# Attention and expert routing in one kernel: expert embedding prepared at the start, idle matmuls redistributed, the last expert's w2 in column halves, the last router on VectorE

## The chip, the cores and the metric

The kernel runs on one core of a Trainium2 chip. A core has a matrix engine (TensorE, "PE" in the profile, with its weight loads as "PEld"), VectorE ("DVE"), ScalarE ("ACT"), GpSimd ("POOL") and SyncE ("SP", which here only issues transfers), and 16 DMA engines that serve all of them. Each engine runs its own list of instructions in order and waits on semaphores for the others. The metric is the device time of one execution in microseconds; the number for a kernel is the median of its runs.

## What is computed

The reference is an attention with an extra 1 in the softmax sum, followed by a layer of eight experts of which every token uses one:

```python
batch, n_heads, seq, head_dim = 8, 12, 448, 64          # attention
N, D, E, F = 3584, 768, 8, 1024                          # tokens, width, experts, hidden

scores = scale * np.matmul(q, k.transpose(0, 1, 3, 2))
m = np.max(scores, axis=-1, keepdims=True)
e = np.exp(scores - m)
attn = e / (np.sum(e, axis=-1, keepdims=True) + np.exp(-m) + 1e-09)
x = np.matmul(attn, v)                                   # then (B, S, H*D), flattened to (N, D)

xn = x / (np.linalg.norm(x, axis=-1, keepdims=True) + 1e-06)
en = expert_emb / (np.linalg.norm(expert_emb, axis=-1, keepdims=True) + 1e-06)
logits = xn @ en.T / tau
expert_idx = np.argmax(logits, axis=1)                   # one expert for each token
# gate_w = softmax(logits) at expert_idx
out[mask] = gate_w[mask, None] * (np.maximum(x[mask] @ w1[e], 0.0) @ w2[e])   # for each e
```

All inputs are float32. For each batch of 448 tokens the kernel finds the expert that most of its tokens chose, fetches only that expert's w1 and w2 (GpSimd's DMA casts them to bf16) and computes the whole batch with it. Tokens that chose another expert are handled afterwards by a loop that is entered only if there are any; with these inputs nothing of it shows in the profile.

## The kernel before

Heads are handled in pairs, 6 pairs for a batch, 48 in all. The program is written as a list of pieces of work, each put at a position; a pair has a slot of 8 positions (`NSLOT = 8`). The pieces are sorted by position, and so the order of the instructions on each engine follows. Attention runs alone for the first eleven slots; from then on the experts of a finished batch are computed between the matmuls of the later pairs. Nothing is left to overlap with the last batch's expert.

The constants and the expert embedding. `prep_expert_emb` is called at position 4 and `prep_expert_emb_t` in slot 5; the scaled embedding is needed when the first batch is routed, in slot 7:

```python
    emb = k.wp.tile([E, DM], F32, name="emb_raw", tag="w1")
    nc.sync.dma_start(emb[:], k.emb[:, :])
    ss = k.csp.tile([E, 1], F32, name="emb_ss", tag="cs")
    nrm = k.csp.tile([E, 1], F32, name="emb_nrm", tag="cs")

    def sq():
        sq = k.wp.tile([E, DM], F32, name="emb_sq", tag="w1")
        nc.scalar.activation(sq[:], emb[:], ACT.Square, accum_out=ss[:])

    def root():
        nc.gpsimd.tensor_tensor(out=nrm[:], in0=ss[:], in1=k.half[0:E, 0:1], op=ALU.pow)

    def ens():
        nc.vector.tensor_scalar_add(nrm[:], nrm[:], 1e-6)
        rs = k.csp.tile([E, 1], F32, name="emb_rs", tag="cs")
        nc.vector.reciprocal(out=rs[:], in_=nrm[:])
        nc.vector.tensor_scalar_mul(rs[:], rs[:], 1.0 / float(tau))
        k.ens = k.wp.tile([E, DM], F32, name="emb_scaled", tag="w1")
        nc.vector.tensor_scalar_mul(k.ens[:], emb[:], rs[:])

    k.en = k.const.tile([128, NP, 32], F32, name="en")
    k.put(s + 19.9, lambda: nc.vector.memset(k.en[:], 0.0))
    k.put(s + 20.8, sq)
    k.put(s + 24.5, root)
    k.put(s + 34.9, ens)


def prep_expert_emb_t(k, s):
    nc = k.nc
    tp = k.work.tile([128, 512], F32, name="work", tag="work")
    for c in range(NP):
        nc.tensor.transpose(tp[:, c * E : c * E + E], k.ens[:, 128 * c : 128 * c + 128], k.ident[:E, :E])

    def out():
        nc.vector.tensor_copy(
            out=k.en[:, :, 0:E], in_=tp[:, 0 : NP * E].rearrange("p (c e) -> p c e", e=E)
        )

    k.put(s + 1, out)

```

The first load. `nc.sync` and `nc.scalar` are the two queues that issue it:

```python
    else:   # in load_qk, for the first two pairs
        for h in range(0, 2 * GP, 2):
            for eng, dst, src in ((nc.sync, t.qm, k.q), (nc.scalar, t.km, k.k)):
                for j in range(2):
                    eng.dma_start(dst[:, :, h + j, :], src[0, h + j, 0:SM, :].rearrange("(p t) d -> p t d", t=3))
            for j, src in ((0, k.q), (1, k.k)):
                nc.sync.dma_start(t.r[64 * j : 64 * j + 64, h : h + 2, :], src[0, h : h + 2, SM:S, :].rearrange("h p d -> p h d"))
    k.ld[n] = t
```

The pieces for a pair, with their positions (`scores` makes four blocks of scores, their exp on ScalarE and the subtraction of 1 on VectorE; `attend` is the product with v; `recip` takes 1/(sum + 1) as exp(-ln)), and the idle matmuls, which compute nothing that is used (`warm(k, n)` issues n matmuls of 128x128 by 512 columns):

```python
    for g in range(G):
        s = g * NSLOT
        put(s - NSLOT + 4.2, lambda g=g, s=s - NSLOT + 4.2: front_qk(k, g, s))
        put(s + (0.8 if g else 4.85), lambda g=g: front_v(k, g))
        for j, o, pa, pv in ((0, 0, 0.3, 1.5), (1, 0.05, 0.4, 2.6), (2, 5.2, 6, 7.7), (3, 0.12, 2.3, 2.7 if g else 4.9)):
            put(s + o, lambda g=g, j=j, pa=s + pa, pv=s + pv: scores(k, g, j, pa, pv))

        s += NSLOT
        put(s + 0.1, lambda g=g, s=s: attend(k, g, s + 0.1))
        put(s + 4.75, lambda g=g, s=s: normalise(k, g, s + 4.75))
        put(s + (4.9 if g == G - 1 else NSLOT + 4.26 if on_pool(g) else NSLOT + 2.35), lambda g=g: square(k, g))
        if 0 < g % NP < NP - 1:
            p = not on_pool(g) and g < G - 2
            put(s + NSLOT + (2.6 if g == G - 2 else 4.28 if p else NSLOT + 0.6), lambda g=g, p=p: square_add(k, g, p))
    put(-NSLOT, lambda: warm(k, 15))
    for g in range(LAG):
        for o in (2.8, 5.4):
            put(g * NSLOT + o, lambda: warm(k, 3))
    for b in range(B):
        s = ((b + 1) * NP + 1) * NSLOT
        if b == B - 1:
            last_batch(k, G * NSLOT)
            break
        put(s + 2.85, lambda b=b, s=s: router_mm(k, b, s + 4.65))
        put(s + 5.35, lambda b=b, s=s: router_tok(k, b, s + 6.9))
```

```python
    def recip():   # in attend
        nc.scalar.activation(rd[:], ps[:, :, 0:S], ACT.Ln, bias=1.0, scale=1.0 / (S + 1.0))
        nc.scalar.activation(rd[:], rd[:], ACT.Exp, scale=-1.0)
```

The router of a batch: `router_mm` multiplies x with the embedding and sums the squares, `router_tok` turns the result so that tokens lie on partitions, and then:

```python
    m = p.tile([128, 4], F32, name="m", tag="m")
    nc.vector.reduce_max(out=m[:], in_=l[:], axis=AX.X)

    nc.gpsimd.tensor_tensor(out=l[:], in0=l[:], in1=m[:].unsqueeze(2).broadcast_to([128, 4, E]), op=ALU.subtract)
    oh = p.tile([128, 4, E], F32, name="oh", tag="oh")
    nc.gpsimd.tensor_scalar(out=oh[:], in0=l[:], scalar1=0.0, scalar2=None, op0=ALU.is_equal)
    ohb = p.tile([128, 4, E], BF16, name="ohb", tag="ohb")
    nc.gpsimd.tensor_tensor(out=ohb[:], in0=oh[:], in1=k.mask[:], op=ALU.mult)
    k.ohb[b], k.lg[b] = ohb, (l, nrm)
```

`router_pick` counts the tokens of each expert with a matmul of ones by `ohb`, `router_count` finds the most frequent expert, `router_index` loads its number into a register of GpSimd, and `fetch` loads a piece of the weights:

```python
def w_piece(k, e0, i):
    if i < 3:
        ...   # a piece of w1
    else:
        w = k.wp.tile([128, 2, DM], BF16, name="w2", tag="w2", bufs=8)
        src = k.w2[bass.ds(e0, 1), :, :].rearrange("o (f p) m -> p (o f) m", p=128)[:, 2 * i - 6 : 2 * i - 4, :]
    k.nc.gpsimd.dma_start(w[:], src)
    return w
```

The last batch fetches w1 in four column blocks (`fetch_columns`) and w2 by `fetch`, in four row blocks of 256 rows each. A hidden block is `moe_h` (6 matmuls for one of 8 blocks of 128 hidden units), an output tile is `moe_y` (128 tokens by 384 columns, 8 matmuls, one for each hidden block) or `moe_yr` (the last 64 tokens, both column halves, 16 matmuls):

```python
        nc.tensor.matmul(   # in moe_y
            ps[:, 0:SM], lhsT=hs[f][:, 128 * t : 128 * t + 128], rhs=w2[f // 2][:, f % 2, SM * n : SM * n + SM],
            start=(f == 0), stop=(f == NF - 1),
        )
    # ... the order of a batch's pieces, in moe_chunks:
    return [h(f) for f in range(NF)] + [y(0, 0), y(0, 1), yr, y(1, 0), y(1, 1), y(2, 0), y(2, 1)]
```

```python
def last_batch(k, s):
    # cut: b, put
    at = [s + o for o in (-5.2, -2.7, -2.6, 0.5, 1.0, 1.5, 5.5, 6.5)] + [s + 7.5 + 0.5 * i for i in range(22)]
    out = {0: (s - 3.4, True), 1: (s - 1.0, False), 2: (s + 0.5, True), 3: (s + 0.95, True), 4: (s + 2.5, False),
           5: (s + 4.8, True), 6: (s + 5.9, True), 7: (s + 6.6, False)}
    for i, fn in enumerate(moe_chunks(k, b - 1, s + 13.5) + moe_chunks(k, b)):
        put(at[i], lambda fn=fn, l=out.get(i, (at[i] + 0.45, i % 2 == 1)): fn(*l))
    # ... router_mm at s + 5.0 to router_index at s + 7.2
    for i in range(4):
        put(s + 7.3, lambda i=i: fetch_columns(k, b, i))
        put(s + 7.9, lambda i=i: fetch(k, b, 3 + i))
    # ... the rest of the gate
```

## Time and profile before

| | |
|---|---|
| time, median of 3 runs | 401.76 us (400.56 to 402.38) |
| span of the profiled execution | 400.7 us |
| TensorE, VectorE, ScalarE, GpSimd busy | 96%, 76%, 75%, 53% |
| data moved by DMA | 69.74 MB, mean 174 GB/s |
| chain that ended last, by engine | PE 75%, DVE 12%, POOL 4%, DMA 3%, issue 3%, ACT 2% |

How to read it. "L287" is line 287 of the kernel. A line of the timeline gives the start, the duration (of all instructions merged into the line), engine, source line, operation, output and inputs by name, and in brackets how long the engine had been idle before it and what released it. In the slices each digit is a fortieth of the span (10 us) in tenths; PEclk is the granted clock of TensorE. The costliest groups of the page are the exp of the scores (ScalarE, 144 instructions of 917 ns), the subtraction of 1 (VectorE, 144 of 631 ns) and the matmuls of the experts (384 of 326 ns and 336 of 356 ns; consecutive matmuls overlap).

### The profile page before, as it was taken

Reading aid. Unit: us, or ns where it says so; the run is one execution under the profiler, and the core shown is the slowest. Engines: PE = TensorE matmul, PEld = TensorE weight load, DVE = VectorE, ACT = ScalarE, POOL = GpSimd, SP = SyncE. Lnnn points to the kernel's source line nnn. Section 1 sums busy time; section 2 is a strip of 40 time slices with the busy share of each in tenths; the row PEclk is TensorE's granted clock in tenths of the full one; section 3 lists DMA queues with packets and bytes.
Section 4 is the critical chain, followed back from the end, with each engine's and each line's share of the span. In section 5 each row is a group of like instructions: output and inputs, shape, how many; then the busy total and the mean of one; then the engine's idle time right before and its main releaser. Section 6 shows DMA issues by size and latency. Waiting matters only on the chain.

```text
span 400.7 us, 7192 instructions
## 1 busy us (share of the span) xinstructions
PE 383.0 (96%) x2303; PEld 238.9 (60%) x2303; DVE 305.2 (76%) x678; ACT 299.2 (75%) x438; POOL 210.6 (53%) x302
## 2 busy tenths in 40 slices
PE   7999999899999999999999999999999999999975
PEld 3565565565666656665666656765666656655533
DVE  2789979967978878887978878887888888762311
ACT  1898889677888788787887887887887887852211
POOL 1423339943677248752776258651876349624800
PEclk9999999789999999999999999999999999999999
DMA  5878648998399959999499949999599808952993
GB/s 129 198 180 203 153 108 164 203 186 173 61 232 241 214 126 175 244 213 216 97 217 245 234 100 187 262 197 224 91 235 217 188 2 152 215 89 37 189 247 122
DMA packets 135688, 69.74 MB, mean 174 GB/s; under 512 B 99544, under 2 KB 130264, under 8 KB 135648
## 3 DMA queue, kind: packets, MB, share of 16 engines
q1 hardware_dynamic: 115344, 43.69, 43.1%
q0 software_dynamic: 18704, 25.17, 38.7%
q10 hardware_dynamic: 1600, 0.39, 0.4%
q8 instruction: 19, 0.31, 0.3%
q14 instruction: 21, 0.17, 0.2%
HBM read 83.39 MB, written 16.52 MB: 249 GB/s over the span
## 4 chain that ended last, share of the span: by engine, by line
PE 75%; DVE 12%; POOL 4%; DMA 3%; issue 3%; ACT 2%; POOLq 0%; DVEq 0%
PE work L528 16%; PE work L558 14%; PE av L287 12%; PE big L243 9%; DVE x L309 4%; PE tq L202 4%; PE work L249 4%; PE rmm L353 3%; PE tk L202 3%; DMA w<-in_moe_w_dram 3%; PE work L684 3%; PE work L577 2%; PE av L278 2%; DVE qt L213 2%; ACT e L254 1%
## 5 line engine op out<-in xcount | busy, mean ns | idle before, releaser
L254 ACT ACTIVATE e<-big 128x896 f32<-128x896 f32 x144 | 126.4, 917 | 30.3 <-PE big L243 29.9
L262 DVE TENSOR_SCALAR em<-e 128x896 fp32r<-128x896 f32 x144 | 89.5, 631 | 9.9 <-ACT e L254 6.9
L558 PE MATMUL work<-w,h 128*128 128x384 bf16 x384 | 68.6, 326 | 3.6 <-DMA w<-in_moe_w_dram 2.7
L528 PE MATMUL work<-xb,w 128*128 128x448 bf16 x336 | 71.4, 356 | 0.3 <-DVE h L537 0.3
L309 DVE SCALAR_TENSOR_TENSOR x<-av,rd 64x448 f32<-64x448 f32 x96 | 66.3, 691 | 2.9 <-ACT rd L296 0.7
L287 PE MATMUL av<-em,vab 128*128 128x448 f32 x288 | 67.6, 370 | 0.0
L243 PE MATMUL big<-qt,kt 64*128 64x448 f32 x288 | 58.3, 441 | 3.7 <-DVE kt L217 2.1
L287 PEld LDWEIGHTS av<-em,vab 128*128 128x128 f32 x288 | 54.8, 191 | 4.5 <-DVE em L262 0.4
L191 POOL TENSOR_TENSOR vs<-vs,vld 128x256 f32<-128x256 f32 x48 | 35.6, 742 | 37.3 <-ACT xs L334 19.1
L558 PEld LDWEIGHTS <-h 128*128 128x128 bf16 x384 | 36.0, 100 | 30.3 <-issue 9.8
L295 ACT ACTIVATE rd<-av 128x896 f32<-128x896 f32 x48 | 44.4, 925 | 6.9 <-PE av L292 6.4
L528 PEld LDWEIGHTS <-w 128*128 128x128 bf16 x336 | 31.7, 103 | 29.7 <-issue 6.7
L296 ACT ACTIVATE rd<-rd 128x896 f32<-128x896 f32 x48 | 45.7, 952 | 1.5
L537 DVE TENSOR_SCALAR h<-work 128x448 bf16<-128x448 f32 x45 | 28.1, 625 | 24.1 <-PE work L528 22.7
L213 DVE CAST qt<-tq 128x448 fp32r<-128x448 f32 x48 | 29.7, 618 | 20.2 <-PE tq L204 20.0
L191 POOL TENSOR_TENSOR vs<-vld 128x256 f32<-128x256 f32 x24 | 18.4, 768 | 49.8 <-PE av L292 33.0
L481 POOL DMA_DIRECT2D w<-in_moe_w_dram x53 | 41.3, 779 | 6.1 <-DVE h L537 2.7
L243 PEld LDWEIGHTS big<-qt,kt 64*128 64x128 f32 x288 | 24.2, 184 | 31.8 <-ACT e L254 10.1
L548 DVE TENSOR_SCALAR y<-work,g 128x384 f32<-128x384 f32 x31 | 19.2, 618 | 26.3 <-PE work L558 20.2
L550 ACT ACTIVATE y<-work,g 128x384 f32<-128x384 f32 x25 | 14.5, 581 | 25.1 <-PE work L558 20.6
L209 ACT CAST kt<-tk 128x384 fp32r<-128x384 f32 x48 | 22.4, 468 | 12.8 <-PE tk L202 12.8
L341 POOL TENSOR_TENSOR acc<-acc,xs 128x448 f32<-128x448 f32 x24 | 27.2, 1135 | 0.9 <-DVE emx L265 0.9
(108 smaller groups left out, 565.0 us busy)
## 6 DMA issues: line engine op xcount, KB each, us to landing
w<-in_moe_w_dram POOLq DMA_DIRECT2D x32, 384.0 KB, 6.5
w<-in_moe_w_dram POOLq DMA_DIRECT2D x21, 512.0 KB, 7.3
vld<-in_v_dram SPq DMA_DIRECT2D x24, 384.0 KB, 5.7
out_dram<-y SPq DMA_DIRECT2D x48, 192.0 KB, 6.1
qm<-in_q_dram SPq DMA_DIRECT2D x69, 128.0 KB, 3.8
km<-in_k_dram SPq DMA_DIRECT2D x69, 128.0 KB, 5.4
vld<-in_v_dram SPq DMA_DIRECT2D x48, 32.0 KB, 4.7
out_dram<-y SPq DMA_DIRECT2D x16, 96.0 KB, 6.5
```

What stands on the lines that cost most here:

```text
L191: k.behind(nc.gpsimd.tensor_tensor(out=vs[:], in0=(vs[:] if j > 1 else t.v[:, :, 0, :]), in1=t.v[:, :, j, :], op=ALU.add))
L213: nc.vector.tensor_copy(out=qt[:], in_=pq[:, 0:S])
L243: nc.tensor.matmul(ps[:, h, 0:S], lhsT=kt[64 * h : 64 * h + 64, 128 * j : 128 * j + 128], rhs=qt[64 * h : 64 * h + 64, :], start=True, sto ...
L254: nc.scalar.activation(e[:], ps[:, :, 0:S], ACT.Exp, scale=scale)
L262: k.last = nc.vector.tensor_scalar_sub(em[:], e[:], 1.0)
L287: nc.tensor.matmul(ps[:, h, 0:S], lhsT=va[:, j, h : h + 2, :], rhs=k.ems[g, j][:, h, :], start=False, stop=(j == 2),)
L295: nc.scalar.activation(rd[:], ps[:, :, 0:S], ACT.Ln, bias=1.0, scale=1.0 / (S + 1.0))
L296: nc.scalar.activation(rd[:], rd[:], ACT.Exp, scale=-1.0)
L309: nc.vector.scalar_tensor_tensor(out=x[r, :], in0=ps[r, h, 0:S], scalar=ps[r, 0, S : S + 1], in1=rd[o, h, :], op0=ALU.add, op1=ALU.mult,)
L481: k.nc.gpsimd.dma_start(w[:], src)
L528: nc.tensor.matmul(ps[:, 0:S], lhsT=(w1[c // 2][:, c % 2, 128 * f : 128 * f + 128] if len(w1) == 3 else w1[f // 2][:, c, 128 * (f % 2) : 1 ...
L558: nc.tensor.matmul(ps[:, 0:SM], lhsT=hs[f][:, 128 * t : 128 * t + 128], rhs=w2[f // 2][:, f % 2, SM * n : SM * n + SM], start=(f == 0), st ...
```

## The change

It touches the irregular places of the schedule and leaves the rest alone.

- The expert embedding is loaded at the very start by GpSimd's queue, and its norm, scaling and transposition are done in slots -1 and 0, while the first loads land, instead of in slots 3 to 5. Its constants are set earlier.
- One of the first loads (the remainder of k, rows 384 to 447) moves from SyncE's to ScalarE's queue.
- Idle matmuls: 10 in place of 15 at the start; none in slot 0 at the place where the embedding is now transposed; none in slot 7, where the first router runs; 8 in place of 3 in the second place of slot 10, just before the first expert starts.
- In slot 0 the second subtraction of 1 goes behind the next pair's copies.
- For the last pair `recip` works on each head by itself; the squares of the last two pairs are put earlier.
- For the last batch the router's three operations for the one-hot of the best expert run on VectorE in place of GpSimd.
- For the last batch w2 is fetched as (column half, row half) in place of four row blocks, and the output tiles of the first column half come first.

The diff, with cuts marked:

```diff
--- before.py
+++ after.py
@@ -41,6 +41,10 @@
     make_identity(nc, k.ident[:])
     k.ones_f = pool.tile([128, 1], F32, name="ones_f")
     nc.vector.memset(k.ones_f[:], 1.0)
+    k.half = pool.tile([128, 4], F32, name="half")
+    nc.vector.memset(k.half[:], 0.5)
+    k.en = pool.tile([128, NP, 32], F32, name="en")
+    nc.vector.memset(k.en[:], 0.0)
     iota_i = pool.tile([128, E], I32, name="iota_i")
     nc.gpsimd.iota(iota_i[:], pattern=[[1, E]], base=0, channel_multiplier=0)
     row_i = pool.tile([128, 1], I32, name="row_i")
# cut: two hunks that only take k.half out of its old place; further down, the one that uses w2_part in moe_yr
@@ -100,7 +102,7 @@
 def prep_expert_emb(k, s):
     nc, tau = k.nc, k.tau
     emb = k.wp.tile([E, DM], F32, name="emb_raw", tag="w1")
-    nc.sync.dma_start(emb[:], k.emb[:, :])
+    nc.gpsimd.dma_start(emb[:], k.emb[:, :])
     ss = k.csp.tile([E, 1], F32, name="emb_ss", tag="cs")
     nrm = k.csp.tile([E, 1], F32, name="emb_nrm", tag="cs")
 
@@ -119,11 +121,9 @@
         k.ens = k.wp.tile([E, DM], F32, name="emb_scaled", tag="w1")
         nc.vector.tensor_scalar_mul(k.ens[:], emb[:], rs[:])
 
-    k.en = k.const.tile([128, NP, 32], F32, name="en")
-    k.put(s + 19.9, lambda: nc.vector.memset(k.en[:], 0.0))
-    k.put(s + 20.8, sq)
-    k.put(s + 24.5, root)
-    k.put(s + 34.9, ens)
+    k.put(s + 0.5, sq)
+    k.put(s + 0.6, root)
+    k.put(s + 4.8, ens)
 
 
 def prep_expert_emb_t(k, s):
@@ -137,7 +137,7 @@
             out=k.en[:, :, 0:E], in_=tp[:, 0 : NP * E].rearrange("p (c e) -> p c e", e=E)
         )
 
-    k.put(s + 1, out)
+    k.put(s + 2.15, out)
 
 
 def load_qk(k, n):
@@ -163,8 +163,8 @@
             for eng, dst, src in ((nc.sync, t.qm, k.q), (nc.scalar, t.km, k.k)):
                 for j in range(2):
                     eng.dma_start(dst[:, :, h + j, :], src[0, h + j, 0:SM, :].rearrange("(p t) d -> p t d", t=3))
-            for j, src in ((0, k.q), (1, k.k)):
-                nc.sync.dma_start(t.r[64 * j : 64 * j + 64, h : h + 2, :], src[0, h : h + 2, SM:S, :].rearrange("h p d -> p h d"))
+            for j, eng, src in ((0, nc.sync, k.q), (1, nc.sync if h else nc.scalar, k.k)):
+                eng.dma_start(t.r[64 * j : 64 * j + 64, h : h + 2, :], src[0, h : h + 2, SM:S, :].rearrange("h p d -> p h d"))
     k.ld[n] = t
 
 
@@ -292,8 +292,11 @@
         nc.tensor.matmul(ps[:, 0, S : S + 1], lhsT=k.va[g // GP][:, 2 * i : 2 * i + 2, :], rhs=k.ones_f[:], start=True, stop=True)
 
     def recip():
-        nc.scalar.activation(rd[:], ps[:, :, 0:S], ACT.Ln, bias=1.0, scale=1.0 / (S + 1.0))
-        nc.scalar.activation(rd[:], rd[:], ACT.Exp, scale=-1.0)
+        parts = (slice(0, 1), slice(1, 2)) if g == B * NP - 1 else (slice(0, 2),)
+        for h in parts:
+            nc.scalar.activation(rd[:, h, :], ps[:, h, 0:S], ACT.Ln, bias=1.0, scale=1.0 / (S + 1.0))
+        for h in parts:
+            nc.scalar.activation(rd[:, h, :], rd[:, h, :], ACT.Exp, scale=-1.0)
 
     k.put(s + 0.04, rest)
     k.put(s + 2.3, recip)
@@ -380,11 +383,12 @@
     m = p.tile([128, 4], F32, name="m", tag="m")
     nc.vector.reduce_max(out=m[:], in_=l[:], axis=AX.X)
 
-    nc.gpsimd.tensor_tensor(out=l[:], in0=l[:], in1=m[:].unsqueeze(2).broadcast_to([128, 4, E]), op=ALU.subtract)
+    eng = nc.vector if b == B - 1 else nc.gpsimd
+    eng.tensor_tensor(out=l[:], in0=l[:], in1=m[:].unsqueeze(2).broadcast_to([128, 4, E]), op=ALU.subtract)
     oh = p.tile([128, 4, E], F32, name="oh", tag="oh")
-    nc.gpsimd.tensor_scalar(out=oh[:], in0=l[:], scalar1=0.0, scalar2=None, op0=ALU.is_equal)
+    eng.tensor_scalar(out=oh[:], in0=l[:], scalar1=0.0, scalar2=None, op0=ALU.is_equal)
     ohb = p.tile([128, 4, E], BF16, name="ohb", tag="ohb")
-    nc.gpsimd.tensor_tensor(out=ohb[:], in0=oh[:], in1=k.mask[:], op=ALU.mult)
+    eng.tensor_tensor(out=ohb[:], in0=oh[:], in1=k.mask[:], op=ALU.mult)
     k.ohb[b], k.lg[b] = ohb, (l, nrm)
 
 
@@ -494,6 +498,20 @@
     k.wts[b][0].append(w)
 
 
+def fetch_halves(k, b, i):
+    w = k.wp.tile([128, NF // 2, SM], BF16, name="w2c", tag="w2", bufs=8)
+    src = k.w2[bass.ds(k.e0[b], 1), :, :].rearrange("o (f p) m -> p (o f) m", p=128)
+    n, j = i // 2, i % 2
+    k.nc.gpsimd.dma_start(w[:], src[:, NF // 2 * j : NF // 2 * (j + 1), SM * n : SM * n + SM])
+    k.wts[b][1].append(w)
+
+
+def w2_part(w2, f, n):
+    if w2[0].shape[2] == SM:
+        return w2[2 * n + f // (NF // 2)][:, f % (NF // 2), :]
+    return w2[f // 2][:, f % 2, SM * n : SM * n + SM]
+
+
 def keep_rows(k, b):
 
     nc = k.nc
@@ -556,7 +574,7 @@
     ps = k.work.tile([128, 512], F32, name="work", tag="work")
     for f in range(NF):
         nc.tensor.matmul(
-            ps[:, 0:SM], lhsT=hs[f][:, 128 * t : 128 * t + 128], rhs=w2[f // 2][:, f % 2, SM * n : SM * n + SM],
+            ps[:, 0:SM], lhsT=hs[f][:, 128 * t : 128 * t + 128], rhs=w2_part(w2, f, n),
             start=(f == 0), stop=(f == NF - 1),
         )
 
@@ -626,6 +644,8 @@
                lambda n, y: send(s + 1, k.out[b * S + SM : b * S + S, SM * n : SM * n + SM], y),
                lambda fn: k.put(s, fn), vec)
 
+    if b == B - 1:
+        return [h(f) for f in range(NF)] + [y(0, 0), y(1, 0), y(2, 0), yr, y(0, 1), y(1, 1), y(2, 1)]
     return [h(f) for f in range(NF)] + [y(0, 0), y(0, 1), yr, y(1, 0), y(1, 1), y(2, 0), y(2, 1)]
 
 
@@ -700,7 +720,7 @@
     put(s + 7.2, lambda: router_index(k, b))
     for i in range(4):
         put(s + 7.3, lambda i=i: fetch_columns(k, b, i))
-        put(s + 7.9, lambda i=i: fetch(k, b, 3 + i))
+        put(s + 7.9, lambda i=i: fetch_halves(k, b, i))
     put(s + 7.4, lambda: router_first(k, b))
     put(s + 7.5, lambda: router_pow(k, b))
     put(s + 7.6, lambda: router_exp(k, b))
@@ -732,8 +752,8 @@
     k.hev = {}
     k.behind = behind
     put(4.6, lambda: build_late_consts(k))
-    put(4, lambda: prep_expert_emb(k, 4))
-    put(5 * NSLOT + 2.7, lambda: prep_expert_emb_t(k, 5 * NSLOT + 2.7))
+    put(-NSLOT, lambda: prep_expert_emb(k, -NSLOT))
+    put(2.8, lambda: prep_expert_emb_t(k, 2.8))
     for n in range(NG * B):
         s = n * GP * NSLOT
         put(max(-NSLOT, s - 6 * NSLOT + 5.2), lambda n=n: load_qk(k, n))
@@ -747,20 +767,21 @@
         s = g * NSLOT
         put(s - NSLOT + 4.2, lambda g=g, s=s - NSLOT + 4.2: front_qk(k, g, s))
         put(s + (0.8 if g else 4.85), lambda g=g: front_v(k, g))
-        for j, o, pa, pv in ((0, 0, 0.3, 1.5), (1, 0.05, 0.4, 2.6), (2, 5.2, 6, 7.7), (3, 0.12, 2.3, 2.7 if g else 4.9)):
+        for j, o, pa, pv in ((0, 0, 0.3, 1.5), (1, 0.05, 0.4, 2.6 if g else 4.86), (2, 5.2, 6, 7.7), (3, 0.12, 2.3, 2.7 if g else 4.9)):
             put(s + o, lambda g=g, j=j, pa=s + pa, pv=s + pv: scores(k, g, j, pa, pv))
 
         s += NSLOT
         put(s + 0.1, lambda g=g, s=s: attend(k, g, s + 0.1))
         put(s + 4.75, lambda g=g, s=s: normalise(k, g, s + 4.75))
-        put(s + (4.9 if g == G - 1 else NSLOT + 4.26 if on_pool(g) else NSLOT + 2.35), lambda g=g: square(k, g))
+        put(s + (4.9 if g == G - 1 else NSLOT + (4.26 if on_pool(g) else 0.3 if g == G - 2 else 2.35)), lambda g=g: square(k, g))
         if 0 < g % NP < NP - 1:
             p = not on_pool(g) and g < G - 2
-            put(s + NSLOT + (2.6 if g == G - 2 else 4.28 if p else NSLOT + 0.6), lambda g=g, p=p: square_add(k, g, p))
-    put(-NSLOT, lambda: warm(k, 15))
+            put(s + NSLOT + (0.9 if g == G - 2 else 4.28 if p else NSLOT + 0.6), lambda g=g, p=p: square_add(k, g, p))
+    put(-NSLOT, lambda: warm(k, 10))
     for g in range(LAG):
         for o in (2.8, 5.4):
-            put(g * NSLOT + o, lambda: warm(k, 3))
+            if g != NP + 1 and (g, o) != (0, 2.8):
+                put(g * NSLOT + o, lambda n=(8 if (g, o) == (LAG - 1, 5.4) else 3): warm(k, n))
     for b in range(B):
         s = ((b + 1) * NP + 1) * NSLOT
         if b == B - 1:
```

## The prediction, made before the changed kernel ran

> **What bounds the kernel now.** I read the page first (busy shares and the 40 slices), then the chain of waits in order of time, then the timeline of five stretches that the change touches. TensorE is busy 96% of the span and carries 75% of the chain, but a share says nothing of a stage, so I split the span by the `Ln` instruction (line 295), which runs once per head pair. Its starts in the timeline of ScalarE give the pace: 16.73, 22.39, 28.24, 33.84, 40.10, 46.47, 52.12, 59.56, 65.63, 71.30, 80.22, 89.15, then a steady cycle of six pairs in 44.65 us (89.15 to 133.80, 133.80 to 178.43). So there are three regimes: attention alone up to about 72 us at 5.66 us a pair, a disturbed handover, and from 89 us the mixed steady state. The change leaves the steady state alone; it touches irregular places only.
>
> The slices show the handover as the only place where the clock drops:
>
> ```profile
> PE   7999999899999999999999999999999999999975
> PEclk9999999789999999999999999999999999999999
> ```
>
> The windows put it at 0.66 of full clock from 74 to 80 us:
>
> ```profile
> 68.00:74.00 6.00, 5.66 (x31) 3.54 (x30) 5.89 (x12) 5.68 (x9) 5.59 (x6) 1.00 1.10 227
> 74.00:80.00 6.00, 4.36 (x15) 3.34 (x16) 5.63 (x13) 2.65 (x4) 5.76 (x9) 0.66 1.09 200
> ```
>
> (columns: length, then PE, PEld, DVE, ACT, POOL busy, clock, DMA share, GB/s: DVE and POOL are full before the clock falls.) The timeline, start and duration first, bracket = idle before and releaser, carries the rest:
>
> ```profile
> 1.67 6.36 PE L684 MATMUL work<-ident 128*128 128x512 bf16 x15 [1.67 <-POOL ident masks.py:199]
> 5.95 0.62 SPq L167 DMA_DIRECT2D qkrest<-in_q_dram  x1
> 7.87 0.49 PE L202 MATMUL tq<-ident,qm 128*128 128x128 f32 x3
> ...
> 38.08 0.61 DVE L120 TENSOR_SCALAR emb_scaled<-emb_raw,emb_rs 8x768 f32<-8x768 f32 x1
> 39.32 0.55 ACT L256 ACTIVATE e<-work 128x448 f32<-128x448 f32 x1 [0.75 <-DVE em L262]
> ...
> 51.94 0.81 PE L684 MATMUL work<-ident 128*128 128x512 bf16 x3
> 55.01 0.62 DVE L213 CAST qt<-tq 128x448 fp32r<-128x448 f32 x1 [1.98 <-PE tq L204]
> ...
> 74.97 0.67 PE L243 MATMUL big<-qt,kt 64*128 64x448 f32 x4 [1.12 <-DVE kt L217]
> 76.31 0.74 PE L278 MATMUL av<-emx,vab 64*128 64x448 f32 x2 [0.67 <-DVE x L309]
> 77.52 2.44 PE L287 MATMUL av<-em,vab 128*128 128x448 f32 x6
> 80.04 2.40 PE L528 MATMUL work<-xb,w 128*128 128x448 bf16 x6
> ...
> 364.29 0.18 PE L444 MATMUL pick<-ohb,ones_b 128*128 128x32 bf16 x1 [0.22 <-POOL ohb L387]
> 372.19 2.76 PE L558 MATMUL work<-w,h 128*128 128x384 bf16 x16 [0.56 <-DVE y L548]
> 385.03 0.48 PE L558 MATMUL work<-w,h 128*128 128x384 bf16 x2 [0.34 <-DMA w<-in_moe_w_dram]
> 387.88 1.79 PE L558 MATMUL work<-w,h 128*128 128x384 bf16 x10 [2.37 <-DMA w<-in_moe_w_dram]
> ```
>
> The reader is to see: the 15 idle matmuls end just when the first transpose starts; the embedding work makes ScalarE wait; in the router's slot VectorE waits for a TensorE that runs idle matmuls; six L287 matmuls take 2.44 us where they otherwise take 1.39; and the last expert waits 2.7 us for w2.
>
> [...] an idle matmul takes 0.43 us in the first 6 us and 0.22 us later, and the half-clock stretch runs from 76.3 to about 82.8 us. [...] The trace has 0.62 us per issue on SyncE, so that is what moving one load can save directly. [...] The trace: 0.23, 0.31, 0.25 us on GpSimd against 0.15 to 0.2 for the small VectorE operations beside them.
>
> **The change part by part.**
>
> Start. Five idle matmuls at 0.427 us are 2.1 us; they end at 1.67 + 10 x 0.427 = 5.94 instead of 8.03. The loads for the first transposes are issued by 3.31 us (the key remainder last) and land 3 us later, about 6.2; on ScalarE's queue the key remainder goes out third, about 2.4, so all land by about 5.8. The transposes can begin near 6.0, 1.9 us earlier. [...] In the old order the second query remainder went out only at 5.95; in the new one it waits for the very first load and should go out about 4.6. So the next group's loads move by 1 to 1.5 us and do not eat up the gain. Against it: squaring the embedding now stands in front of the first key copy on ScalarE. GpSimd's memsets end at 2.46, issue 0.8, landing about 3 us later gives 6.3; the square takes some 0.65 us and the first key copy slips by about 0.2. Then GpSimd's power (1.04), four VectorE operations (37.54 to 38.69 before, 1.15 us) and six tiny transposes (0.53) come before the second pair's transposes, whose own release (the first exp) is at about 9.1; they start about 9.75. Net: -1.5.
>
> Embedding out of slots 3 to 5. VectorE loses 1.15 us plus the 0.21 us copy. The gaps between `Ln` from 28.24 to 46.47 are 18.23 us against 3 x 5.66 = 16.98: 1.25 too long; a 0.48 us memset there stays. ScalarE's square no longer lies in a full slot (5.85 against 5.66). Net: -1.1.
>
> Router's first slot. Six idle matmuls go, 0.65 us of TensorE per three. The first triple stands directly ahead of the router matmuls and the transposes for which VectorE waits 1.98 us: worth 0.65. The second triple stands before scores for which ScalarE waits 0.72; but after it VectorE runs nearly without a gap (55.0 to 66.1), so little passes on. Net: -0.8.
>
> Handover. Five more idle matmuls, 5 x 0.216 = 1.08 us, fill the 1.12 us wait for the key copy, which itself stays since VectorE is late there. If the clock holds, the matmuls from 76.3 to 82.8 are about 3.2 us shorter. But the third piece of w1, issued at 71.92 with 8.8 us to landing, comes about 80.7, and the fifth matmul of the first expert chunk, which needs it, would stand at about 79.4. So over half of it turns into a wait: 81.1 in place of 82.3. Times three chances in four that the clock holds, rounded up for what follows: -1.2.
>
> End. The three one-hot operations end 0.5 us sooner on VectorE, so the pick wait of 0.22 goes, the gather of weights starts 0.5 us earlier, and the 0.56 us wait at 372.19 (the y copy stood behind an operation that waited for GpSimd's expert index) mostly goes. Two half-size `Ln`/`Exp` pairs let the first normalise start earlier, 0.25. For w2: the old order needs the third piece at 384.7 and the fourth at 385.5; they came at 385.03 and 387.88. With column halves the first three tiles, 24 matmuls x 0.167 = 4.0 us, need only the first two pieces, and the rest are needed at about 387 to 387.7 on the old scale, where the fourth came at 387.9 less 0.5. The 2.7 us goes, with perhaps 0.3 left. Net: -(0.22 + 0.5 + 0.25 + 2.7) + 0.3 = -3.4.
>
> Sum: 1.5 + 1.1 + 0.8 + 1.2 + 3.4 = 8.0; I take 0.2 off because consecutive gains in the first regime meet three nearly full engines. 401.76 - 7.8 = 394.0.
>
> **The rivals.** (a) The clock stays low at the start: ten idle matmuls are only 4.27 us of work, then 0 to 1.5 us of idleness. For it: all 15 ran at the slow 0.427. Against: TensorE is never idle for long there. It would give back 1 to 1.5 us: 395.3. (b) The clock still falls at the handover, because the 0.67 us wait and a new wait for w1 lie close together: 395.2. With (a) 396.5. (c) The clock holds and w1 comes in time, because the router ran earlier too: another 1.7 us, 392.3. (d) The w2 halves are read in rows of 1536 bytes in place of 3072, twice as many; if they come later than the old pieces, the wait returns as one in front of the first tile or the remainder: up to 2 us, 396. Nothing in the old trace shows it, though w1's column pieces, in rows of 1024 bytes, landed in 5.2 and 7.5 us. (e) The embedding load lands late and holds the first key copy on ScalarE: 1 us for each us of delay.
>
> **Range and chances.** The steady 270 us do not move, so slower by 2% would need a new fault: 0.02. The 2% line is 393.7, almost at my sum; half of the rivals fall above it. 8 in 10: 391.3 to 397.3. Faster by over 2%: 0.46, within: 0.52.
>
> **What would show it.** First transposes near 6 us; `Ln` of the first pair near 15.2 in place of 16.73; 5.7 us between the `Ln`s up to 50 us; no half clock near 75 us, but TensorE waiting for w1 in the first chunk; no wait for w2 above 0.5 us in the last expert. I am wrong if the first `Ln` has moved less than 0.8 us, if clock 0.7 shows anywhere after 10 us, or if the last 25 us are not 3 us shorter from the last router matmul on.

## The result, and the profile after

The changed kernel takes 397.63 us (median of 4 runs, 395.80 to 398.62) against 402.02 us for the kernel before on the same chip (400.56 to 402.38): a ratio of 0.989, 95% interval 0.985 to 0.994. It is faster, by 1.1%. The prediction said 394.0 us and a range of 391.3 to 397.3.

The profiled executions have spans of 397.0 and 400.7 us. I split the 3.7 us between them at the same instructions as in the prediction: the first `Ln` of each pair on ScalarE, and the first router matmul of the last batch. (That point is meant wherever a text says "the last router matmul".)

| stretch | before | after | difference | predicted |
|---|---|---|---|---|
| start to first `Ln` | 16.73 | 17.73 | +1.0 | -1.5 |
| six pairs (embedding work gone) | 35.39 | 34.32 | -1.1 | -1.1 |
| three pairs with the router's first slot | 19.18 | 18.54 | -0.6 | -0.8 |
| two pairs at the handover | 17.85 | 14.68 | -3.2 | -1.2 |
| from there to the first router matmul of the last batch | 269.58 | 270.00 | +0.4 | 0 |
| from that matmul to the end | 41.97 | 41.73 | -0.2 | -3.4 |

Two middle rows came as predicted. The handover gave more, the start gave nothing, and of the 3.4 us at the end 0.2 came. The slices of the page after the change:

```profile
PE   6999999999999999999999999999999999999975
PEclk9699999999999999999999999999999999999998
```

The dip of the clock at the handover (the two digits 7 and 8 before) is gone; there is a new one in the second slice. The windows at the handover, in the columns of the prediction:

```profile
68.00:74.00 6.00, 5.97 (x33) 3.83 (x33) 5.87 (x13) 5.23 (x8) 5.61 (x6) 1.00 1.14 213
74.00:80.00 6.00, 5.40 (x32) 3.66 (x32) 5.63 (x13) 4.55 (x7) 5.59 (x10) 1.00 1.16 215
```

The clock is 1.00 where it was 0.66, and TensorE runs 32 matmul instructions from 74 to 80 us instead of 15. The timeline, for the places shown before:

```profile
1.85 4.45 PE L704 MATMUL work<-ident 128*128 128x512 bf16 x10 [1.85 <-POOL ident masks.py:199]
4.63 0.62 SPq L167 DMA_DIRECT2D qkrest<-in_q_dram  x1
6.63 0.84 ACT L111 ACTIVATE emb_sq<-emb_raw 8x768 f32<-8x768 f32 x1 [4.37 <-DMA emb_raw<-in_moe_expert_emb_dram]
7.97 0.68 PE L243 MATMUL big<-qt,kt 64*128 64x448 f32 x4 [0.81 <-ACT kt L209]
9.56 0.62 PE L133 MATMUL work<-ident,emb_scaled 8*128 8x8 f32 x6 [0.50 <-DVE emb_scaled L122]
10.11 0.90 PE L202 MATMUL tq<-ident,qm 128*128 128x128 f32 x3
12.47 1.46 PE L704 MATMUL work<-ident 128*128 128x512 bf16 x3
14.65 1.73 ACT L254 ACTIVATE e<-big 128x896 f32<-128x896 f32 x2 [1.15 <-PE big L243]
...
72.32 1.90 PE L704 MATMUL work<-ident 128*128 128x512 bf16 x8
74.15 0.68 PE L243 MATMUL big<-qt,kt 64*128 64x448 f32 x4
77.49 1.29 PE L546 MATMUL work<-xb,w 128*128 128x448 bf16 x6
...
368.02 2.76 PE L576 MATMUL work<-w,h 128*128 128x384 bf16 x16 [0.58 <-DVE y L566]
383.81 0.62 DVE L566 TENSOR_SCALAR y<-work,g 128x384 f32<-128x384 f32 x1 [4.42 <-DMA out_dram<-y]
384.48 2.00 PE L576 MATMUL work<-w2c,h 128*128 128x384 bf16 x8 [2.02 <-DVE y L566]
385.01 0.58 ACT L568 ACTIVATE y<-work,g 128x384 f32<-128x384 f32 x1 [4.57 <-DMA out_dram<-y]
386.41 2.59 PE L595 MATMUL work<-w2c,h 128*64 128x384 bf16 x16
388.93 4.07 PE L576 MATMUL work<-w2c,h 128*128 128x384 bf16 x24
```

The start: the transposes begin at 6.09 instead of 7.87, but TensorE then idles 0.81 and 0.50 us, the granted clock is 0.50 from 9.79 to 16.62 us, and three transposes take 0.90 instead of 0.49 us. ScalarE waits 1.15 us for scores. The handover: eight idle matmuls end where the four score matmuls begin, and the first six expert matmuls take 1.29 instead of 2.40 us, with no wait for w1 in front. The end: TensorE no longer waits for w2. It waits 2.02 us for a PSUM tile, because VectorE, which should empty that tile, has waited 4.42 us for an output buffer that a DMA is still writing out. Behind the wait the 16 matmuls of the remainder tile take 2.59 instead of 1.49 us: the granted clock is 0.50 from 385.26 to 388.67 us.

The output copies come from a pool of 7 buffers, and the 7 tiles of the batch before hold all of them: their writes are put behind the fifth hidden block of the last expert and were issued from 377.2 us on. Already the first copy of the last expert, on VectorE, had to wait for one of these writes, and so had the second, on ScalarE (4.57 us). TensorE could still compute two tiles, because two PSUM tiles take turns, and stopped at its third.

### The profile page after: what moved, and what is told of

It is laid out like the page before. It is cut to its first block, busy times and chain, and to the rows that moved or that the text cites. A ratio compares the mean times of both kernels' runs of the same rounds, so it can differ in the third digit from the quotient of the medians.

```text
span 397.0 us, 7173 instructions
## 1 busy us (share of the span) xinstructions
PE 381.8 (96%) x2294; PEld 238.5 (60%) x2294; DVE 305.3 (77%) x681; ACT 299.2 (75%) x440; POOL 209.9 (53%) x300
## 4 chain that ended last, share of the span: by engine, by line
PE 79%; DVE 10%; POOL 3%; DMA 3%; issue 2%; ACT 2%; ACTq 0%; POOLq 0%; SPq 0%; DVEq 0%
PE work L546 18%; PE work L576 15%; PE av L287 12%; PE big L243 9%; PE tq L202 4%; PE work L249 4%; DVE x L312 4%; PE rmm L356 3%; PE tk L202 3%; PE work L595 3%; PE av L278 2%; DMA out_dram<-y 2%; DVE qt L213 2%; PE work L704 2%; PE tq L204 1%
## 5 line engine op out<-in xcount | busy, mean ns | idle before, releaser
L546 PE MATMUL work<-xb,w 128*128 128x448 bf16 x336 | 70.3, 352 | 0.3 <-DVE h L555 0.3
L243 PE MATMUL big<-qt,kt 64*128 64x448 f32 x288 | 59.7, 449 | 2.3 <-ACT e L254 1.3
L576 PE MATMUL work<-w,h 128*128 128x384 bf16 x336 | 60.2, 326 | 0.9 <-DVE y L566 0.6
L191 POOL TENSOR_TENSOR vs<-vs,vld 128x256 f32<-128x256 f32 x48 | 35.2, 733 | 34.2 <-ACT xs L337 19.1
L297 ACT ACTIVATE rd<-av 128x896 f32<-128x896 f32 (+1 forms) x49 | 44.5, 910 | 7.8 <-PE av L292 7.2
L299 ACT ACTIVATE rd<-rd 128x896 f32<-128x896 f32 (+1 forms) x49 | 45.8, 937 | 1.5
L485 POOL DMA_DIRECT2D w<-in_moe_w_dram x49 | 37.9, 773 | 5.9 <-DVE h L555 2.7
L568 ACT ACTIVATE y<-work,g 128x384 f32<-128x384 f32 x25 | 14.5, 580 | 25.7 <-PE work L576 13.1
```

The lines of the kernel that those rows point to most:

```text
L191: k.behind(nc.gpsimd.tensor_tensor(out=vs[:], in0=(vs[:] if j > 1 else t.v[:, :, 0, :]), in1=t.v[:, :, j, :], op=ALU.add))
L243: nc.tensor.matmul(ps[:, h, 0:S], lhsT=kt[64 * h : 64 * h + 64, 128 * j : 128 * j + 128], rhs=qt[64 * h : 64 * h + 64, :], start=True, sto ...
L297: nc.scalar.activation(rd[:, h, :], ps[:, h, 0:S], ACT.Ln, bias=1.0, scale=1.0 / (S + 1.0))
L299: nc.scalar.activation(rd[:, h, :], rd[:, h, :], ACT.Exp, scale=-1.0)
L546: nc.tensor.matmul(ps[:, 0:S], lhsT=(w1[c // 2][:, c % 2, 128 * f : 128 * f + 128] if len(w1) == 3 else w1[f // 2][:, c, 128 * (f % 2) : 1 ...
L576: nc.tensor.matmul(ps[:, 0:SM], lhsT=hs[f][:, 128 * t : 128 * t + 128], rhs=w2_part(w2, f, n), start=(f == 0), stop=(f == NF - 1),)
```

## The experiments

My theory for the end: the old wait for w2 was replaced by one for the output buffers, behind it stands the late fourth piece of w2, and either one is followed by a half clock. Rivals: w2 in halves is simply no better; or the times between executions move for another reason. For the start: the clock, or the new order of VectorE's work. All ratios are to the kernel before on the same chip. The first four experiments, the next four, the four after them and the last three ran on four different chips, so a difference between medians of different groups is weaker evidence than one within a group.

**More output buffers.**

```diff
-    n.yp = pool("yp", 7)
+    n.yp = pool("yp", 11)
```

> The changed kernel with 11 output buffers in place of 7. Buffer theory (the last expert's output tiles wait for the previous batch's writes to land, since seven buffers are all still in use): the first output copy no longer waits 4.4 us for a write, TensorE's 2.0 us wait for it goes, and the clock stays up in the last 10 us; from the first router matmul to the end 39.5 us in place of 41.7, so about 395.4 us. Transfer theory (the fourth half of w2, landing at 386.0, binds anyway): the wait moves to the remainder tile, which cannot go on before 386.0 where it now starts at 386.4; then the gain is under 0.7 us, 397 us. Mixed: 1.6 us of new wait for w2 inside the remainder tile and 2.2 us earlier end.

Measured: 397.01 us, ratio 0.986 (0.979 to 0.993), not separable from the changed kernel: the transfer theory had said a gain under 0.7 us. The wait for the buffers is gone, and this stands in its place in the timeline of this run:

```profile
382.71 1.00 PE L595 MATMUL work<-w2c,h 128*64 128x384 bf16 x9
386.20 1.02 PE L595 MATMUL work<-w2c,h 128*64 128x384 bf16 x7 [2.49 <-DMA w2c<-in_moe_w_dram]
387.15 5.50 PE L576 MATMUL work<-w2c,h 128*128 128x384 bf16 x24
```

The remainder tile now reaches the fourth piece of w2, the lower half of the second column half, before it is there, waits 2.49 us, and 24 matmuls then take 5.50 instead of 4.07 us (granted clock 0.74 on the mean from 388 to 392 us). One wait was hidden behind the other, nearly equally long.

**w2 by rows again**, everything else as changed.

```diff
-        put(s + 7.9, lambda i=i: fetch_halves(k, b, i))
+        put(s + 7.9, lambda i=i: fetch(k, b, 3 + i))
-    if b == B - 1:
-        return [h(f) for f in range(NF)] + [y(0, 0), y(1, 0), y(2, 0), yr, y(0, 1), y(1, 1), y(2, 1)]
```

> The changed kernel with w2 fetched by rows again and the old order of output tiles. Buffer theory: the halves bought nothing, because the wait for buffers took the place of the wait for w2; the time from the first router matmul to the end stays within 0.7 us of 41.7, so 397.6 us. Rival (the halves gave their 2.7 us and it was lost elsewhere): 2 to 2.7 us slower, 400 us.

Measured: 398.31 us, 0.992 (0.990 to 0.995): within 0.7 us of the changed kernel, intervals overlapping. The waits are those of before, 0.29 and 2.44 us, the second followed by half clock (10 matmuls take 3.20 us; with full clock 1.79 in the kernel before). As it stands in the change, this part bought nothing measurable.

**Three idle matmuls at the handover instead of eight.**

```diff
-                put(g * NSLOT + o, lambda n=(8 if (g, o) == (LAG - 1, 5.4) else 3): warm(k, n))
+                put(g * NSLOT + o, lambda: warm(k, 3))
```

> The changed kernel with 3 idle matmuls in place of 8 at the handover. Clock theory: the clock falls again near 75 us, the Ln of the eleventh and twelfth pairs come 3.2 us later together, 400.8 us. Rival (the handover gained because the router and w1 came earlier, not because of the clock): under 1 us slower, 398.3 us.

Measured: 398.20 us, 0.992 (0.990 to 0.995). By time that is the number of the rival: 0.6 us slower than the changed kernel, with overlapping intervals. In the trace the clock does fall (half clock from 74.1 to 77.5 us), the two pairs take 16.20 instead of 14.68 us, and the timeline has these waits back:

```profile
72.80 0.67 PE L243 MATMUL big<-qt,kt 64*128 64x448 f32 x4 [0.95 <-DVE kt L217]
74.14 0.74 PE L278 MATMUL av<-emx,vab 64*128 64x448 f32 x2 [0.67 <-DVE x L312]
```

In this pair of profiles 1.5 of the 3.2 us go with the eight matmuls, and the other 1.7 have another source. The kernel before with eight and with filled waits, further down, tells more.

**Idle matmuls in the gaps of the start**: 3 before the first scores, 4 before the transposes of the embedding, into PSUM tiles that are overwritten afterwards.

```diff
+        if g == 0 and j == 0:
+            idle(k, ps[:, 0, :], 3)
...
+    idle(k, tp[:], 4)
```

> The changed kernel with seven more idle matmuls in slot 0, written into the tiles that the next real matmuls overwrite: three before the first scores and four before the embedding's transposes, where TensorE stood idle for 0.8 and 0.5 us. Clock theory for the start (the clock fell at about 10 us because TensorE idled between 6 and 10 us): no half-rate matmuls after 7 us, the first Ln near 15.4 in place of 17.73, 395.4 us and less spread between runs. Embedding theory (its square on ScalarE and its four operations on VectorE delay the first pair): the first Ln stays above 17 us, 397.6 us.

Measured: 395.92 us (395.62 to 396.40), 0.987 (0.983 to 0.991). The clock is full in every slice, but the first `Ln` starts at 16.48, where I expected 15.4. Two profiles of the same start without the idle matmuls have it at 16.23, so filling saved the clock and hardly moved the start. What is left stands in the timeline of ScalarE:

```profile
13.96 1.73 ACT L257 ACTIVATE e<-big 128x896 f32<-128x896 f32 x2 [1.14 <-DVE em L265]
```

The exp of the second pair waits for a subtraction on VectorE, which frees the exp's buffer; the change put the first pair's second subtraction behind the copies of the next pair.

**The embedding back in its old place**, with only the 3 matmuls before the first scores.

```diff
-    put(-NSLOT, lambda: prep_expert_emb(k, -NSLOT))
-    put(2.8, lambda: prep_expert_emb_t(k, 2.8))
+    put(4, lambda: prep_expert_emb(k, 4))
+    put(5 * NSLOT + 2.7, lambda: prep_expert_emb_t(k, 5 * NSLOT + 2.7))
```

(cut: its load on SyncE, its three inner times and the three idle matmuls of slot 0 go back as well.)

> The run with idle matmuls in slot 0, but the embedding prepared in its old place (SyncE's load, slots 3 to 5), and three idle matmuls again in slot 0 where its transposes stood. Embedding theory: the first Ln comes near 15.0 in place of 16.48, since the square no longer stands before the first key copy and the four VectorE operations no longer before the second pair; then 1.0 to 1.2 us are lost again by the seventh Ln, so the total stays within 0.7 us of 395.9. Rival (a load or the clock holds the start): first Ln still above 16 us.

Measured: 397.25 us, 0.989 (0.983 to 0.995), not separable by time from the run before it. In the trace the first `Ln` comes at 16.01, not near 15.0: still above 16, as the rival said, and 0.47 us earlier than in the run before it (0.2 to 0.6 against the three profiles with this filled start). And the next six pairs take 1.15 us more (35.43 against 34.28). Moving the embedding saves 1.15 us in its old slots, as predicted, and costs some 0.5 us in its new one, by single profiles; it is not free there.

**The second subtraction back at its old time**, on top of the idle matmuls in the start.

```diff
-(1, 0.05, 0.4, 2.6 if g else 4.86)
+(1, 0.05, 0.4, 2.6)
```

> The run with idle matmuls in slot 0, with the second subtraction of 1 of slot 0 back ahead of the next pair's copies. e-buffer theory (ScalarE's exp for the second pair waits 1.14 us for that subtraction, because three e buffers are in use): the wait goes, the first Ln comes 0.7 to 0.9 us earlier, near 15.7, 395.1 us. Rival (the move is what lets the key copy go early, and undoing it costs as much): first Ln between 16.2 and 16.9, 395.9 us.

Measured: 395.10 us, 0.983 (0.978 to 0.989). The first `Ln` starts at 15.43, 1.05 us earlier, and the wait of the exp has shrunk to 0.46 us (timeline of ScalarE):

```profile
13.26 1.73 ACT L257 ACTIVATE e<-big 128x896 f32<-128x896 f32 x2 [0.46 <-DVE en L137]
```

This is the 15.2 of the prediction, nearly: the change as written gave it away by its own reordering. Over all profiles with the filled start, those of the later experiments included, the first `Ln` lies at 16.24, 16.48 and 16.58 with the subtraction behind the copies, and at 15.15, 15.43, 15.81 and 16.14 with it back: 0.8 us on the mean. The times of the two runs do not separate.

**Clearing the DMA queue before w2.** First the copy of the last batch's expert input to memory is held until the last hidden block (with 11 buffers and the idle matmuls in the start), then the output writes of the batch before as well:

```diff
+    if b == B - 1:
+        k.behind(ins, k.hev[b, NF - 1])
```

> The run with idle matmuls in slot 0, with 11 output buffers, and the last batch's write of its tokens to memory (688 KB) held until the last hidden block. Contention theory (the fourth half of w2 is late because output writes and this write share the DMA engines with it): the fourth half comes 1 to 2 us earlier than in the run with 11 buffers, TensorE's wait for it is 0.5 to 1.5 us in place of 2.49, from the first router matmul to the end 39 us, 394.9 us. Rival (its own rows of 1536 bytes make it late): the wait stays above 2 us, 395.9 us or more.

```diff
-                k.behind(ins, k.hev[b + 1, NF // 2])
+                k.behind(ins, k.hev[b + 1, NF - 1])
```

(cut: the time at which they are put moves along.)

> As the run before, with the previous batch's output writes also held until the last hidden block in place of the fifth. Contention theory: no wait for w2 above 0.5 us; from the first router matmul to the end 38 us, 394 us, unless the fifth output tile now waits for a buffer (up to 1 us). Rival: the wait for the fourth half stays above 2 us.

Measured: 395.78 us, 0.983 (0.978 to 0.990), with a wait of 1.97 us for w2 left, so holding the copy alone ended near the rival's "above 2 us"; then 394.00 us, 0.979 (0.974 to 0.984), with no wait, as the contention theory said. How long the fourth piece of w2 took from issue to landing tells what changed. In the changed kernel (lines on the tile of w2; the slowest is the fourth piece):

```profile
DMA to landing us min/median/max: 7.9/11.8/15.1
```

With 11 buffers it took 14.5 us. With the copy held too it was issued at 371.4, and TensorE waited for it until 385.4, 14.0 us later:

```profile
385.42 0.81 PE L600 MATMUL work<-w2c,h 128*64 128x384 bf16 x7 [1.97 <-DMA w2c<-in_moe_w_dram]
```

With the output writes held as well, the last of the four issues is at 371.6:

```profile
L508 POOL DMA_DIRECT2D w2c<-in_moe_w_dram x4: 752/760/839, 369.3 to 371.6; - x4
```

Its landing is not recorded, but the tenth matmul of the remainder tile, which needs it, starts without a wait at about 383.4, so it took 11.9 us at most, at least 2 us less than in the profile before it. The size of the effect is uncertain, because other profiles of the changed end with nothing held have 11.6 to 13.7 us. In this profile, with the writes of SyncE's queue held too, the load issued on GpSimd's queue landed sooner than in the one before it; how the queues share the DMA engines is not shown. In the timeline of the kernel with all writes held, the last product runs through:

```profile
378.63 4.06 PE L581 MATMUL work<-w2c,h 128*128 128x384 bf16 x24
382.63 1.49 PE L600 MATMUL work<-w2c,h 128*64 128x384 bf16 x16
384.05 4.07 PE L581 MATMUL work<-w2c,h 128*128 128x384 bf16 x24
```

From the first router matmul of the last batch to the end of the last matmul it takes 33.9 us, against 37.7 both before and after the change.

**All of it together** (idle matmuls in the start, the subtraction, 11 buffers, held writes).

> The changed kernel with all that the earlier runs showed to help: idle matmuls before the first scores and before the embedding's transposes, the second pair's subtraction back at its old place, 11 output buffers, and the writes of the batch before last and of the last batch's input copy held until the last hidden block. Theory (start and end are independent terms): first Ln near 15.4 us as with the subtraction back, last router matmul to end near 38.2 us as with the writes held, so a span near 391.3 and a time near 393.0. Rival (the earlier starts only push work into a later wait): one of the two gains is lost, 394.0 or above.

Measured: 393.44 us (392.25 to 393.90), 0.980 (0.976 to 0.983). First `Ln` at 15.81 (15.4 expected), 33.9 us from the first router matmul of the last batch to the last matmul. The time is within 0.5 us of the theory, and the trace has both gains. But against the kernel before on its own chip it is no better than the run with all writes held (0.979), so that the earlier start reaches the total is not shown by time. From this version I took back two parts of the change.

**w2 by rows in that version** (the edit of the second experiment).

> The run before it with the last w2 by rows and in the old order of tiles. Theory (the halves were worth their saving all along, and only the output buffers and the DMA traffic hid it): the row pieces make the last product wait again, 1.5 to 2.5 us slower than the halves. Rival (with the writes out of the way the rows land in time as well): under 0.5 us of difference.

Measured: 394.45 us, 0.985 (0.980 to 0.990); the intervals overlap. The timeline has the difference:

```profile
377.85 1.23 PE L581 MATMUL work<-w,h 128*128 128x384 bf16 x6
380.09 1.78 PE L581 MATMUL work<-w,h 128*128 128x384 bf16 x10 [1.00 <-DMA w<-in_moe_w_dram]
```

The last row piece still comes 1.00 us late, and the stretch to the last matmul is 35.2 instead of 33.9 us. The halves are worth 1.3 us in this trace and 1.0 us in the medians, less than the 1.5 to 2.5 of the theory, and only once the other waits are gone.

**The last router on GpSimd in that version.**

```diff
-    eng = nc.vector if b == B - 1 else nc.gpsimd
+    eng = nc.gpsimd
```

> The best version with the last router's operations back on GpSimd. Theory (the chain from the last router matmul to the w1 gather is on the path): 0.5 to 0.7 us slower, and from the last router matmul to the end 38.8 instead of 38.2 us. Rival (the gather's landing hides it): no difference.

Measured: 392.89 us, 0.979 (0.975 to 0.983): no difference in time. In the trace the wait of 0.22 us ahead of the pick is back and the last matmul comes 0.35 us later after the router; that is too small for these runs.

**The kernel before with eight idle matmuls at the handover.**

```diff
-            put(g * NSLOT + o, lambda: warm(k, 3))
+            put(g * NSLOT + o, lambda n=(8 if (g, o) == (LAG - 1, 5.4) else 3): warm(k, n))
```

> The kernel before, with nothing changed but 8 idle matmuls at the handover. Theory (the handover gain is the clock, and stands without the rest of the change): 1.5 to 3.2 us faster than before, with the granted clock full from the handover on. Rival (the gain needed the earlier loads of the changed kernel; w1 comes late here): under 1 us.

Measured: 402.34 us against 402.33, ratio 1.001 (0.999 to 1.003). The time says no gain, so the rival seems right; but the trace has both. The handover takes 16.01 instead of 17.85 us, with a granted clock of 1.00 from 66 to 86 us, and the first router matmul of the last batch comes 1.85 us earlier, at 356.88. From there to the last matmul it then takes 2.1 us more, in the timeline of TensorE:

```profile
80.28 0.55 PE L528 MATMUL work<-xb,w 128*128 128x448 bf16 x2 [0.98 <-DMA w<-in_moe_w_dram]
...
384.06 0.48 PE L558 MATMUL work<-w,h 128*128 128x384 bf16 x2 [1.23 <-DMA w<-in_moe_w_dram]
386.58 3.36 PE L558 MATMUL work<-w,h 128*128 128x384 bf16 x10 [2.04 <-DMA w<-in_moe_w_dram]
```

The last line ran at a granted clock of 0.50 (387 to 390 us); in the profile of before it took 1.79 us, after a wait of 2.37 us, at a clock of 1.00. So a wait of the same kind is once followed by half clock and once not. The first line shows the wait for w1 that the prediction feared at the handover.

**Idle matmuls in the waits of the end**, in the kernel before (3 ahead of the third piece of w2, 8 ahead of the fourth), then with the eight at the handover too, then in the changed kernel (8 ahead of its third output tile). The core of the edit:

```diff
     for f in range(NF):
+        if f in gap:
+            idle(k, gap[f])
         nc.tensor.matmul(
```

> The kernel before, with idle matmuls where the last product waits for w2: 3 ahead of its third piece and 8 ahead of its fourth, into a PSUM tile that nothing reads. They take the place of the two waits of 0.34 and 2.37 us. Theory (after a wait of about 2 us the clock falls in some executions and not in others, and that is the end's share of the spread): the executions of the kernel before whose clock fell there become faster by 1.5 to 2 us, the others stay or lose up to 0.3 where the idle matmuls overrun, so 0.3 to 1 us on the median. Rival (the clock falls at the handover alone): no gain.

> The same idle matmuls at the end, and 8 at the handover. Theory (8 idle matmuls at the handover do bring the last router matmul 1.85 us forward, and the clock that then falls behind the w2 wait takes it back): now the gain arrives, 399.0 to 400.5, 1.5 us or more under the run with the idle matmuls at the end alone, with no granted clock below 0.9 in the last 20 us. Rival (w2's landing is set by something that doesn't move with the handover): the wait grows by what the handover gained, no more than 0.5 us under it.

> The changed kernel, with 8 idle matmuls into a PSUM tile that nothing reads ahead of its third tile of the last product, which waits 2.0 us for an output buffer. Theory (the wait costs twice: 2.0 us by itself and 1.3 to 1.9 us by the half clock behind it): 1.3 to 1.9 us faster than the changed kernel, 395.7 to 396.3, with the clock full from there on and the wait itself still there, filled. Rival (executions of the changed kernel mostly keep their clock there): under 0.5 us.

Measured: 400.91 us, 0.998 (0.995 to 1.000), a gain of about 1 us that just clears the noise; 399.82 us, 0.993 (0.990 to 0.996); 395.51 us, 0.982 (0.979 to 0.986). With the end kept busy, the handover's eight matmuls are worth 1.1 us (intervals that just touch), short of the 1.5 I asked for; and that kernel is 0.7% faster than before, where without the filled end it was equal. So a good part of the lost 1.85 us had gone into the clock at the end (3.36 us for ten matmuls instead of 1.79). In the changed kernel the median falls from 397.63 to 395.51, on another chip; in the profiles the stretch to the end takes 40.2 instead of 41.7 us, and these 1.5 us lie in the theory's 1.3 to 1.9. Its timeline:

```profile
380.64 1.89 PE L704 MATMUL big<-ident 128*128 128x512 bf16 x8
382.52 1.46 PE L578 MATMUL work<-w2c,h 128*128 128x384 bf16 x8
383.92 1.61 PE L597 MATMUL work<-w2c,h 128*64 128x384 bf16 x16
385.45 4.07 PE L578 MATMUL work<-w2c,h 128*128 128x384 bf16 x24
```

The wait is nearly as long as it was, now filled; the tile behind takes 1.46 instead of 2.00 and the remainder 1.61 instead of 2.59 us, and the six executions lie within 0.8 us of each other.

The kernel before filled at the end also had a handover of 16.09 us in its profile, at full clock (1.00 from 66 to 86 us), with the old three idle matmuls. So the dip at the handover, which the prediction read as a property of the kernel, is there in one execution and absent in another of the same instructions at that place. With the eight matmuls as well, the old kernel took 14.98 us, nearly the 14.68 of the changed one. The difference is w1, in the first expert chunk of these two:

```profile
79.90 0.55 PE L528 MATMUL work<-xb,w 128*128 128x448 bf16 x2 [1.05 <-DMA w<-in_moe_w_dram]
...
77.60 1.41 PE L528 MATMUL work<-xb,w 128*128 128x448 bf16 x6
```

The third piece of w1 took 8.4 us from issue to landing in the first and 7.3 in the second. So two things decide the handover, the clock and w1: it takes 17.85 us with half clock from 75.9 to 82.8 us, about 16 with full clock and a wait of 1 us for w1 (the eight matmuls help nothing there: 16.01 and 16.09), and under 15 with full clock and w1 in time. In the twelve other profiles of kernels made from the changed one, TensorE waited for w1 only once, for 0.25 us. Why w1 lands sooner in the changed kernel (6.2 us in its profile, 8.8 before) is open.

## Why the prediction was right or wrong

**Start (-1.5): wrong.** The idle matmuls let the transposes begin early and the loads moved up (the second query remainder at 4.63 instead of 5.95), as said. The step that failed here: I wrote that the second subtraction goes behind the copies without pricing it: it holds an exp buffer and costs 1.05 us in one pair of profiles, 0.8 on the mean of seven (shown by putting it back). The half clock, my rival (a), came in three of five profiles with this start, from 9.8, 10.2 and 11.2 us on; with it the first `Ln` came at 17.73, 16.23 and 16.88, without it at 16.54 and 16.23, so it is part of the loss in some executions and not its main cause. Over five profiles with the changed start and no filling, the first `Ln` lies between 16.23 and 17.73; over four with the old start, between 15.89 and 16.74. On the whole nothing was gained.

**Embedding (-1.1): right**, -1.07 in its old slots. That it costs 0.5 us in the new place was part of the start term, too small there.

**Router's first slot (-0.8): right**, -0.64.

**Handover (-1.2): right in mechanism, mis-sized.** The clock held (1.00 from 68 to 80 us). The term that failed is the wait for the third piece of w1: I carried over its 8.8 us to landing; it landed 6.2 us after issue, and nothing waited. Rival (c) of the prediction said 1.7 us more; it was 2.0. Yet 1.8 of the 3.2 us is a clock dip that the old handover does not always have, so the pair of profiles overstates the gain; without the dip it took 16.09.

**End (-3.4): the step that failed.** "The 2.7 us goes, with perhaps 0.3 left" rested on w2 alone. I asked which w2 piece each tile needs, and not where each tile is written to. The waits for w2 went; a wait of 2.02 us for one of 7 output buffers came, followed by about 1.6 us lost to half clock (0.54 on the first tile and 1.1 on the remainder). Rival (d), late w2 pieces, was right too, and stood behind: 2.49 us with more buffers. Both the shape of the pieces and the traffic bear on it. By rows the last piece took 11.1 to 11.7 us to land in five profiles, as halves 11.6 to 15.1 in seven; with the writes held the rows took 9.3, the halves 11.9 at most. (The prediction's 7.5 us for a piece of w1 is a middle value: 5.2, 6.8 and 8.2 are recorded.)

The pair of profiles understates the end: the one before kept its clock there and the one after did not. With the same end, idle matmuls in the start only, three profiles kept it and took 40.1, 39.6 and 40.1 us, 2 us less than before, although the wait for a buffer stayed; one of them:

```profile
382.99 1.46 PE L579 MATMUL work<-w2c,h 128*128 128x384 bf16 x8 [1.87 <-DVE y L569]
```

With all of it cleared the stretch lost 3.8 us to the last matmul, close to the 3.4 predicted. The 0.56 us wait for the y copy stayed (0.58), and the router on VectorE gave 0.35 us in the trace instead of the 0.22 + 0.5. The half-size `Ln`/`Exp` gave nothing of their 0.25: the first router matmul comes 3.32 us after the last pair's first `Ln`, as before. The 0.4 us that the steady stretch lost is spread over 36 pairs and unexplained.

Of my three marks for being wrong, all came true: the first `Ln` did not move forward, clock below 0.7 showed after 10 us, and the end was not 3 us shorter.

Why the clock falls in one execution and not in another of the same kernel: the traces show at least when it changes. In the profile of the changed kernel the granted clock changes at 6.38, 9.79, 16.62, 385.26, 388.67 and 395.50 us, all whole multiples of 3.41 us apart. In that of the kernel before it changes at 7.67, 75.94, 82.76 and 400.20 us, again whole multiples of 3.41 us apart, on a grid in another place. The half clock of the run with three idle matmuls at the handover lasts one such step too, 74.1 to 77.5 us. I call one step of such a grid a window. A wait of about 2 us can fall into one window or be shared by two. These are windows of the grid in the last product, one of the changed kernel, one of the kernel with 1.87 us shown above, and two of the kernel before:

```profile
381.84:385.26 3.42, 1.40 (x9) 0.74 (x8) 0.62 (x1) 0.25 (x1) 0.00 (x0) 1.00 1.08 339
381.27:384.69 3.42, 1.70 (x12) 0.93 (x13) 0.82 (x2) 0.58 (x1) 0.00 (x0) 1.00 1.03 347
383.13:386.55 3.42, 2.04 (x11) 0.96 (x10) 0.43 (x1) 0.54 (x1) 0.00 (x0) 1.00 1.09 224
386.55:389.96 3.41, 2.08 (x16) 1.14 (x17) 0.62 (x1) 0.21 (x1) 0.00 (x0) 1.00 0.80 292
```

TensorE is busy for 1.40 us of the first, and a clock of 0.50 follows; it is busy for 1.70 us or more of the others, and the clock stays at 1.00. In the kernel before the 2.37 us lie across two windows. In the last product, over all profiles, half clock followed the windows with a busy share of 0.14 to 0.41 (five) and none with 0.50 or more. At the start and the handover windows with 0.53 to 0.71 were followed by half clock (the changed kernel from 6.38 to 9.79 us with 2.10 us busy, the kernel before from 72.52 to 75.94 us with 2.00) and others with 0.62 to 0.79 were not, so this share is not the whole measure. No run here set the place of the grid: that it decides is my reading of the traces and not shown by an experiment.

## What to carry to other kernels

Before pricing a wait that a change removes, follow the same tiles one step further: to the buffer they are written to and to the transfers that free it, because an engine stalled by one wait hides the next, and here three stood behind each other (w2, output buffers, w2 again). A late load near the end may be helped by holding the writes that run beside it; here the fourth piece of w2 took 11.9 us at most instead of 14.0, and TensorE waited for no half of w2 in the three profiles that did so. A TensorE wait of about 2 us can cost twice, once by itself (here 2.02 us) and once by the clock behind it (about 1.6 us); here idle matmuls into an unused PSUM tile took the second cost away (1.46 and 1.61 us for the two tiles behind it instead of 2.00 and 2.59). And a single pair of profiles can mistake a clock dip of one execution for a property of the kernel: more profiles of the same stretch tell them apart.
